# A second level of seven products for the down projection, and the next block's attention normed during the up phase

## The chip, the cores and the metric

The kernel runs on one core of a Trainium2 chip. Its measure is device time in microseconds; 1023.92 us is the median of three runs before the change.

## What is computed

Linear attention over 8 batches and 8 heads, then a gated feed-forward layer over all 4608 tokens.

```python
# q, k, v: (8, 8, 576, 64); x: (4608, 512); w_gate, w_val: (512, 1536); w_out: (1536, 512)
kv = np.einsum('bhsd,bhse->bhde', k, v)
o = np.einsum('bhsd,bhde->bhse', q, kv)
o = o / np.sqrt(np.mean(o * o, axis=-1, keepdims=True) + 1e-06) * g_norm
x = o.transpose(0, 2, 1, 3).reshape(4608, 512)
g = x @ w_gate
out = (g * (1.0 / (1.0 + np.exp(-g))) * (x @ w_val)) @ w_out
```

Everything is float32.

## The kernel before, in words

The 4608 tokens are worked in NB = 9 blocks of 512, numbered 0 to 8. A block has an up phase (x times w_gate and w_val, giving the hidden h, 1536 columns) and a down phase (h times w_out). Both use a seven-product scheme (Winograd's form of Strassen's): a 2x2 block product takes 7 block matmuls instead of 8, for additions of blocks on the other engines. The products are numbered 1 to 7. `CHAIN` says into which PSUM bank each goes: 1, 6, 7 and 4 add up one after another in one tile of pool b, each partial sum being copied out before the next product is added; 5 and 3 share a tile of pool c; 2 has pool a. The pools have 3, 2 and 1 banks, and pool m has the last 2, for attention.

From block DEEP = 2 on the up phase uses the scheme twice, an outer 7 of an inner 7 (class `Inner`). It goes through the 1536 hidden columns in three thirds d = 0, 1, 2. A third is four units, one for each group of outer products (`GROUPS`: 1 and 5; 6 and 2; 7; 4 and 3), so there are 12 units; each runs the inner products 1, 5, 6, 2, 7 and, while the next unit has begun, 3 and 4. Results of the first group leave PSUM by ScalarE copies or VectorE additions, those of the other groups by VectorE additions alone (L111 in the profile, the helper `add`). `made3` ends a third: two multiplications make h (L113), and `h_sums` makes the sums that the down phase needs, on GpSimd for d = 0 and 1, on VectorE for d = 2.

Weight combinations of the up phase that are not kept in SBUF were written to DRAM in block 1. The class `Stream` brings them back through a pool of nine t tiles (`t_pool`): `pump` issues a load on SP's queue whenever the ninth tile back has been used. `use` and `free` count the uses.

The down phase (class `Down`) uses one level: 7 products of 12 matmuls, 128x256 each (L565, the matmul of `Quad`). Three of its weight combinations are made on GpSimd into t tiles (`turn_t`, L112 t<-wo), nine operations a block. 

The next block's attention is done alongside. `kv` (L316) runs at one third and two thirds of the up phase. `turn` transposes q on VectorE (L331) after the up phase; `steps` gives what is done after which down product. For block 1 and later: after product 1, `whole`, which is the products q times kv (`heads`, L361), squares on ScalarE (L374), reductions on VectorE (L375), an inverse root of small VectorE operations (`root`, L381 to L393), `scale` (L113 r<-m,y) and the 32x32 transposes of `blocks_x` (L420); after product 5, `place_x`, 16 DMAs with 128-byte rows (L434), 8 on SP's queue and 8 on ScalarE's; after product 2, `gain_x` on ScalarE (L441) and `sums` on VectorE (L111, L112 on x and xi). Loads of k, v and q for the block after the next are issued on SP's queue; q of one block is 32 DMAs of 128-byte rows (L284).

Results and intermediate blocks of 128x2048 share five `ring()` buffers; x, xi, h and s1 have one buffer each. The text gives each engine's work an order of preference, and the Tile scheduler lays out every engine's list in advance: the first instruction in the text whose inputs and buffers it expects to be ready goes next. [...]

## Time and profile before

| | before |
|---|---|
| median of 3 runs | 1023.92 us (1023.57 to 1023.99) |
| profiled execution, first to last instruction (span) | 1021.4 us |
| TensorE busy | 1006.0 us, 98% |
| VectorE busy | 701.1 us, 69% |
| GpSimd busy | 369.0 us, 36% |
| ScalarE busy | 227.9 us, 22% |
| DMA, mean over the span | 167 GB/s |
| one block, 2 to 5, start of down to start of next down | 107.8 us |

The profile is of one execution; the profiled execution's own time is its span, with what lies before the first and after the last instruction outside it. Engines: PE is TensorE's matmul side, PEld its weight loads, DVE VectorE, ACT ScalarE, POOL GpSimd, SP the queue that issues most DMAs. In a row of the time line stand the start in us, the time, the engine, the line, the operation, what is written and read, shapes and the number of merged instructions; in brackets the idle time before it and what ended it. The chain of work that ended last gives start, time and engine. The clock granted to TensorE is full throughout.

### The profile page before, as it was taken

The page shows a single profiled execution, that of the slowest core. Times are in us where ns is not written, and L with a number is a line of the kernel's source. Part 1 is how long each engine was busy: PE and PEld are TensorE (multiplying, and loading weights), DVE is VectorE, ACT ScalarE, POOL GpSimd, SP SyncE. Part 2 cuts the span into 40 slices and gives each one's busy share as a digit, 9 for nine tenths or more (in the row PEclk, how much of TensorE's full clock was granted, in tenths as well). Part 3 has the DMA queues.
Part 4 walks back from the last instruction along what each step waited for, and adds up shares of the span by engine and source line. Part 5 has one row for each costly group of instructions (what it writes and reads, how often), then busy time and mean ns, then how long its engine had stood idle before and what let it go on. Part 6 is the DMA issues. An engine that isn't in the chain of part 4 may idle for free.

```text
span 1021.4 us, 21409 instructions
## 1 busy us (share of the span) xinstructions
PE 1006.0 (98%) x8522; PEld 897.1 (88%) x8522; DVE 701.1 (69%) x1169; ACT 227.9 (22%) x353; POOL 369.0 (36%) x280
## 2 busy tenths in 40 slices
PE   6999999999999999999999999999999999999998
PEld 4544688888999989998999899988998999989997
DVE  2999688998665946685558566665669466946661
ACT  2765112121211221121121211111121211221110
POOL 0000263534055503561246315630555045513670
PEclk9999999999999999999999999999999999999999
DMA  8689643767888377845686568636772766066601
GB/s 237 203 255 271 124 77 108 187 165 156 250 210 255 60 176 203 252 92 129 209 238 144 96 195 247 177 60 201 231 199 46 177 195 190 22 167 201 191 27 42
DMA packets 273845, 170.26 MB, mean 167 GB/s; under 512 B 150609, under 2 KB 241873, under 8 KB 273745
## 3 DMA queue, kind: packets, MB, share of 16 engines
q1 hardware_dynamic: 238800, 164.42, 59.3%
q10 hardware_dynamic: 34880, 4.46, 2.7%
q8 instruction: 68, 1.11, 0.4%
q14 instruction: 33, 0.26, 0.1%
q0 software_dynamic: 64, 0.00, 0.0%
HBM read 138.02 MB, written 22.41 MB: 157 GB/s over the span
## 4 chain that ended last, share of the span: by engine, by line
PE 90%; DVE 6%; DMA 2%; issue 1%; ACT 1%; SPq 0%; DVEq 0%; ACTq 0%
PE b L728 26%; PE b L565 19%; PE c L728 13%; PE c L565 10%; PE a L728 6%; PE a L565 5%; PE b L1032 4%; PE c L1032 4%; PE m L316 2%; PE m L361 1%; DVE r L112 1%; DVE xi L112 1%; DVE r L111 1%; DMA h<-in_v_dram 1%; DVE t L112 1%
## 5 line engine op out<-in xcount | busy, mean ns | idle before, releaser
L111 POOL TENSOR_TENSOR r<-r 128x256 f32<-128x256 f32 (+1 forms) x105 | 110.8, 1061 | 300.9 <-DVE r L111 272.2
L111 DVE TENSOR_TENSOR r<-b,r 128x512 f32<-128x512 f32 (+1 forms) x273 | 161.9, 606 | 65.5 <-PE b L728 60.1
L112 POOL TENSOR_TENSOR t<-wo 128x512 f32<-128x512 f32 x81 | 114.5, 1438 | 212.4 <-DVE wo L111 102.9
L111 DVE TENSOR_TENSOR r<-c,r 128x512 f32<-128x512 f32 (+1 forms) x179 | 108.5, 617 | 89.0 <-PE c L728 54.8
L728 PE MATMUL b<-x,t 128*128 128x128 f32 x1092 | 151.3, 276 | 0.0
L111 DVE TENSOR_TENSOR r<-a,r 128x512 f32<-128x512 f32 (+1 forms) x99 | 62.5, 631 | 113.4 <-PE a L565 70.7
L728 PEld LDWEIGHTS b<-x,t 128*128 128x128 f32 x1092 | 136.5, 192 | 0.8
L728 PE MATMUL c<-xi,t 128*128 128x128 f32 x840 | 112.4, 276 | 0.4 <-DVE xi L111 0.4
L113 POOL TENSOR_TENSOR h<-r 128x1024 f32<-128x1024 f32 (+1 forms) x40 | 82.3, 2072 | 76.9 <-DVE r L111 73.9
L728 PEld LDWEIGHTS c<-xi,t 128*128 128x128 f32 x840 | 102.9, 192 | 0.5 <-DVE xi L111 0.5
L565 PE MATMUL b<-wo,h 128*128 128x256 f32 x432 | 100.1, 383 | 0.1
L565 PE MATMUL b<-t,h 128*128 128x256 f32 x432 | 96.9, 381 | 0.0
L565 PEld LDWEIGHTS b<-t,h 128*128 128x128 f32 x432 | 81.6, 190 | 11.3 <-issue 0.2
L565 PEld LDWEIGHTS b<-wo,h 128*128 128x128 f32 x432 | 79.9, 190 | 13.1 <-DVE h L113 2.5
L742 ACT COPY r<-b 128x512 f32<-128x512 f32 x63 | 36.9, 585 | 211.6 <-PE b L728 211.6
L728 PE MATMUL b<-xi,t 128*128 128x128 f32 x588 | 79.8, 276 | 0.0
L728 PEld LDWEIGHTS b<-xi,t 128*128 128x128 f32 x588 | 72.4, 192 | 0.0
L728 PE MATMUL b<-x,wg 128*128 128x128 f32 x336 | 52.7, 279 | 0.2 <-DVE x L112 0.2
L728 PE MATMUL b<-x,wv 128*128 128x128 f32 x336 | 51.4, 276 | 0.0
L565 PE MATMUL a<-wo,h 128*128 128x256 f32 x216 | 48.3, 379 | 0.0
L565 PE MATMUL c<-t,s 128*128 128x256 f32 x216 | 48.1, 380 | 0.0
L565 PE MATMUL c<-wo,h 128*128 128x256 f32 x216 | 48.1, 379 | 0.0
(133 smaller groups left out, 1565.7 us busy)
## 6 DMA issues: line engine op xcount, KB each, us to landing
t<-w SPq DMA_DIRECT2D x336, 256.0 KB, 3.6
out_dram<-r SPq DMA_DIRECT2D x17, 512.0 KB, 3.1
ld<-in_k_dram SPq DMA_DIRECT2D x26, 288.0 KB, 5.2
ld<-in_v_dram SPq DMA_DIRECT2D x26, 288.0 KB, 5.9
ld<-in_moe_w_gate_dram SPq DMA_DIRECT2D x12, 512.0 KB, 4.8
ld<-in_moe_w_val_dram SPq DMA_DIRECT2D x12, 512.0 KB, 4.7
ld<-in_moe_w_out_dram SPq DMA_DIRECT2D x12, 512.0 KB, 4.9
w<-t SPq DMA_DIRECT2D x18, 256.0 KB, 3.0
```

The source lines that it names most:

```text
L111: add = lambda e, o, a, b: e.tensor_tensor(out=o, in0=a, in1=b, op=OP.add)
L112: sub = lambda e, o, a, b: e.tensor_tensor(out=o, in0=a, in1=b, op=OP.subtract)
L113: mul = lambda e, o, a, b: e.tensor_tensor(out=o, in0=a, in1=b, op=OP.mult)
L316: nc.tensor.matmul(self.kv_ps[r][u * D : (u + 1) * D, g, :], lhsT=k[:, u, c, :], rhs=v[:, u, c, :], start=(c == 0), stop=(c == KT - 1),)
L361: self.multiplied = nc.tensor.matmul(self.ps[i][u][p : p + D, t, j, :], lhsT=self.qt[rows, 2 * i + t, j, p : p + D], rhs=kvs[b % 3][rows, ...
L565: nc.tensor.matmul(banks[e][:, e], lhsT=lhsT, rhs=rhs, start=first and i == 0 and (e == 0 or banks[0] is not banks[1]), stop=i == self.ste ...
L728: nc.tensor.matmul(ps[:, i, f], lhsT=self.weight(o, p, f), rhs=self.operand(o, p), start=first and (i, f) == (0, 0), stop=True, skip_group ...
L742: nc.scalar.copy(out=dst, in_=ps)
L1032: nc.tensor.matmul(t, lhsT=w[f // 2][:, i, P * (f % 2) : P * (f % 2 + 1)], rhs=x[:, i, of], start=(i == 0), stop=(i == NS - 1),)
```

## The change

With DEEPER = 3, blocks 3 to 8 take the down products by two levels: outer 7 of inner 7, each with three matmuls of 128x128 (over d), 147 in all, in three groups of outer products (1, 2 and 4; 6 and 5; 3 and 7). The class `DeepDown` does it. The operands need more sums of blocks of h (`turn_h`, and `leaf` on VectorE for the first group and on GpSimd for the others); results are put together by VectorE, ScalarE and GpSimd (`row`). Weights: the combinations of the outer products 4, 5 and 7 are made once, on GpSimd in block 2 (`send_t`), written to DRAM and streamed back through the t tiles, 21 loads a block; those of the resident outer products are partly made on GpSimd each time (`get_down`, 12 a block) after wo was prepared in block 3. `turn_t` is not called from block 3 on.

For the next block (4 to 8) `turn` moves to the two-thirds point of up, and the steps of `whole` are split over the last third of up (`early`): the first half's products and root after unit 9 of 12, its scaling and the second half's products and root after unit 10, the second scaling after 11, `blocks_x` after 12. The squares are put into t tiles instead of a ring buffer. `place_x` and `end` stay in the down phase, in the first and the second group.

```diff
-            if i == 0:
+            early = self.n > DEEPER
+            if i == 0 and not early:
                 self.sq = ring().rearrange("p f (t j d) -> p f t j d", t=2, j=NS)
             for u in range(2):
-                sq = self.sq[:, 2 * i + u]
+                if early:
+                    sq = t_tile((self.n, "sq", i, u)).rearrange("p a (t x) -> p (a t x)", t=2)
+                    sq = sq.rearrange("p (t j d) -> p t j d", t=2, j=NS)
+                else:
+                    sq = self.sq[:, 2 * i + u]
                 self.squared = nc.scalar.activation(out=sq, in_=self.ps[i][u], func=ACT.Square)
                 self.summed = nc.vector.tensor_reduce(out=self.z[:, i, u], in_=sq, axis=mybir.AxisListType.X, op=OP.add)
+                if early:
+                    stream.free((self.n, "sq", i, u))
...
+        def early(self):
+            def first():
+                self.product(0)
+                self.root(0)
+            def second():
+                self.scale(0)
+                self.product(1)
+                self.root(1)
+            return {9: first, 10: second, 11: lambda: self.scale(1), 12: self.blocks_x}
...
+            if self.n > DEEPER:
+                return {5: self.place_x, 2: end}
...
+            if self.ffn.n >= DEEPER:
+                self.ffn.turn_h(self.d, engine)
+            else:
+                self.ffn.ended = self.ffn.h_sums(2 * self.d, 2, engine)
...
+    DEEPER = 3
+    DOWN = (((1, 2, 4), (1, 5, 2, 6, 3, 7, 4)), ((6, 5), (1, 5, 6, 3, 2, 7, 4)), ((3, 7), (1, 5, 6, 3, 2, 7, 4)))
+    DOWN_LEAVES = (1, 6, 2, 3, 4, 5, 7)
+    PLACE = {1: (0, 0), 2: (1, 0), 6: (0, 1), 3: (1, 1)}
+    wos = wo.rearrange("p (d m e) (g c x) -> p d m e g c x", m=2, e=2, g=2, c=2)
...
+                if n >= DEEPER:
+                    self.next += [
+                        (n, o, p, None) for os, ps in DOWN for p in ps for o in os
+                        if o not in RESIDENT or p not in QUARTER
+                    ]
...
+                if len(key) == 4:
+                    self.tiles[key] = t_tile(key).rearrange("p l (f c) -> p (l f) c", f=2)
+                    self.uses[key] = NP // 2
+                    self.get_down(self.tiles[key][:, 0 : NP // 2], *key[1:3])
+                    continue
...
+        def get_down(self, to, o, p):
+            if o in RESIDENT:
+                e, g = PLACE[o]
+                m, c = {5: (1, 1), 7: (0, 0), 4: (1, 0)}[p]
+                sub(nc.gpsimd, to, wos[:, :, m, e, g, c], wos[:, :, 0, e, g, 1])
+            else:
+                nc.sync.dma_start(out=to, in_=self.down[o][:, DOWN_LEAVES.index(p)])
...
+        def send_t(self, o):
+            if o == 4:
+                room = s_pool.tile([P, NP, HB], F32, name="s1").rearrange("p j (r t) -> p (j r) t", t=P)
+            else:
+                if o == 5:
+                    self.leaves = x_pool.tile([P, 3, 7, P], F32, name="xi").rearrange("p a b c -> p (a b) c")
+                room = self.leaves[:, 9 * (o == 7) :]
+            e = nc.gpsimd
+            for d in range(NP // 2):
+                t = self.turned_t[o][d].rearrange("p m (c x) -> p m c x", c=2)
+                t2_, to = t[:, 0, 1], room[:, 3 * d : 3 * d + 3]
+                sub(e, t2_, t[:, 1, 1], t2_)
+                add(e, t2_, t2_, t[:, 0, 0])
+                sub(e, to[:, 0:2], t[:, 1], t2_.unsqueeze(1).to_broadcast([P, 2, P]))
+                sub(e, to[:, 2], t[:, 0, 0], t2_)
+                down = stream.down[o]
+                nc.sync.dma_start(out=down[:, 0:4, d], in_=t.rearrange("p m c x -> p (m c) x"))
+                nc.sync.dma_start(out=down[:, 4:7, d], in_=to)
+            stream.free((self.ffn.n, o))
...
+    class DeepDown:
...
+        MADE = {1: (0, 0), 5: (1, 1), 6: (0, 1), 4: (1, 0)}
+        ADDED = {2: (0, 0), 7: (1, 1), 3: (0, 1)}
...
+        def multiply(self, group, p, ds=(0, 1, 2)):
+            outers = DOWN[group][0]
+            name, first = CHAIN[p]
+            if first and ds[0] == 0:
+                self.ps[name] = PSUMS[name].tile([P, 4, P], F32, name=name)
+            ps = self.ps[name][:, 0 : len(outers)]
+            for i, o in enumerate(outers):
+                for d in ds:
+                    nc.tensor.matmul(
+                        ps[:, i], lhsT=self.operand(o, p, d), rhs=self.weight(o, p, d),
+                        start=first and (i, d) == (0, 0), stop=d == 2, skip_group_check=True,
+                    )
+            if ds[-1] == 2:
+                q, c = (self.ADDED if p in self.ADDED else self.MADE)[p]
+                dst = (self.r[:, 0:3], self.r[:, 0:4:3], self.o)[group][:, :, q, c]
+                if p in self.ADDED:
+                    add(nc.vector, dst, ps, dst)
+                elif group == 0:
+                    nc.scalar.copy(out=dst, in_=ps)
+                elif group == 1:
+                    add(nc.vector, dst[:, 0], ps[:, 0], dst[:, 0])
+                    nc.scalar.copy(out=dst[:, 1], in_=ps[:, 1])
+                else:
+                    add(nc.vector, dst, ps, self.r[:, 0:1, q, c].to_broadcast([P, 2, P]))
+            stream.pump()
...
+        def go(self, nxt):
+            fill = nxt.steps() if nxt else {}
+            fill = {k: fill.get(k, lambda: None) for k in (1, 5, 2)}
+            h, r, forms = self.h, self.r, self.forms
+            vector, pool_ = nc.vector, nc.gpsimd
+            final = nxt is None
+            stream.enable(self.n + 1)
+            for p in (1, 5, 2):
+                self.multiply(0, p, (0, 1))
+            self.multiply(0, 1, (2,))
+            with tc.issue_after(self.ffn.ended.ins):
+                self.multiply(0, 2, (2,))
+            self.multiply(0, 5, (2,))
+            room = x_pool.tile([P, 7, 2, HB], F32, name="x").rearrange("p a b (c t) -> p (a b c) t", t=P)
+            for p in (3, 7):
+                to = room[:, 9 * (p == 7) :][:, 0:9].rearrange("p (o d) t -> p o d t", o=3)
+                self.leaf(
+                    vector, p, to[:, 0:2].rearrange("p o d t -> p d o t"), lambda m, q: h[:, :, m, :, 0, q]
+                )
+                self.leaf(vector, p, to[:, 2], lambda m, q: h[:, :, m, 1, 1, q])
+                for i, o in enumerate((1, 2, 4)):
+                    forms[o, p] = to[:, i]
+            self.multiply(0, 6)
+            self.multiply(0, 3)
+            self.row(pool_, add, 1, r[:, 1], r[:, 0], 0)
+            self.s1 = s_pool.tile([P, NP, HB], F32, name="s1")
+            pairs = self.ffn.h.rearrange("p (j e) t -> p e j t", e=2)
+            a11, a12, a21, a22 = (pairs[:, e, :, HB * g : HB * (g + 1)] for g in range(2) for e in range(2))
+            add(vector, self.s1, a21, a11)
+            s1 = self.s1.rearrange("p (d m) (q t) -> p d m q t", m=2, q=2)
+            xi = x_pool.tile([P, 3, 7, P], F32, name="xi").rearrange("p a b c -> p (a b) c")
+            for i, p in enumerate((5, 3, 7)):
+                for k, of in ((6, lambda m, q: h[:, :, m, 0, 1, q]), (5, lambda m, q: s1[:, :, m, q])):
+                    at = 6 * i + 3 * (k == 5)
+                    forms[k, p] = xi[:, at : at + 3]
+                    self.leaf(pool_, p, forms[k, p], of)
+            self.multiply(0, 7)
+            fill[5]()
+            self.multiply(0, 4)
+            self.row(pool_, add, 1, r[:, 1], r[:, 0], 1)
+            if final:
+                self.store(r[:, 1], 0, 0)
+            sub(vector, a11, a21, a22)
+            sub(vector, a12, a12, a21)
+            for p in (1, 5, 6, 3, 2):
+                self.multiply(1, p)
+            self.row(pool_, add, 0, r[:, 0], r[:, 3], 0)
+            fill[2]()
+            self.multiply(1, 7)
+            self.multiply(1, 4)
+            self.row(pool_, add, 0, r[:, 0], r[:, 3], 1)
+            sub(pool_, r[:, 2], r[:, 2], r[:, 3])
+            for p, to in ((5, h[:, :, 0, 1, 1]), (3, h[:, :, 0, 0, 1]), (7, h[:, :, 1, 1, 1])):
+                self.leaf(pool_, p, to, lambda m, q: h[:, :, m, :, 0, q])
+                forms[7, p], forms[3, p] = to[:, :, 0], to[:, :, 1]
+            self.o = self.quads(ring())[:, 0:2]
+            for p in (1, 5, 6, 3, 2):
+                self.multiply(2, p)
+            engine = vector if final else pool_
+            self.row(engine, add, 2, self.o[:, 1], r[:, 2], 0)
+            if final:
+                self.store(self.o[:, :, 0], 0, 1, 2)
+                self.store(r[:, 2, 0:1], 2, 0)
+            self.multiply(2, 7)
+            self.multiply(2, 4)
+            self.row(engine, add, 2, self.o[:, 1], r[:, 2], 1)
+            if final:
+                self.store(self.o[:, :, 1], 1, 1, 2)
+                self.store(r[:, 2, 1:2], 3, 0)
+            else:
+                self.store(self.o.rearrange("p o q c t -> p (o q) c t"), 0, 1)
+                self.store(r[:, 1:3].rearrange("p o q c t -> p (o q) c t"), 0, 0)
...
+        def turn_h(self, d, engine):
+            h = self.h.rearrange("p (d m e) (g q t) -> p d m e g q t", m=2, e=2, g=2, q=2)[:, d]
+            outer = self.h.rearrange("p (j e) t -> p e j t", e=2)[:, :, 2 * d : 2 * d + 2]
+            a11, a21, a22 = outer[:, 0, :, 0:HB], outer[:, 0, :, HB:BLK], outer[:, 1, :, HB:BLK]
+            s2 = h[:, 0, :, :, 1]
+            add(engine, s2, s2, h[:, 1, :, :, 1])
+            sub(engine, s2, s2, h[:, 0, :, :, 0])
+            to = self.s1.rearrange("p j (r t) -> p (j r) t", t=P)[:, 0:9].rearrange("p (o d) t -> p d o t", o=3)[:, d]
+            add(engine, to[:, 0:2], h[:, 0, :, 0, 1], h[:, 0, :, 0, 0])
+            self.ended = add(engine, to[:, 2], h[:, 0, 1, 1, 1], h[:, 0, 1, 1, 0])
+            add(engine, a21, a21, a22)
+            return sub(engine, a21, a21, a11)
...
+            if self.n == DEEPER:
+                for d in range(NP // 2):
+                    of = lambda m, c, d=d: wos[:, d, m, :, :, c]
+                    self.making += [
+                        lambda of=of: sub(nc.gpsimd, of(0, 1), of(1, 1), of(0, 1)),
+                        lambda of=of: add(nc.gpsimd, of(0, 1), of(0, 1), of(0, 0)),
+                    ]
...
+                if self.n == DEEPER - 1 and p in (5, 7, 4):
+                    down.send_t(p)
...
-                nxt.kv(0)
+                with tc.issue_after(ffn.multiplied.ins) if n >= DEEPER else ExitStack():
+                    nxt.kv(0)
                 nxt.load_kv(1)
             def two_thirds():
                 nxt.kv(1)
+                if n >= DEEPER:
+                    nxt.turn()
...
+            if nxt and n >= DEEPER:
+                fill.update(nxt.early())
             ffn.up(fill)
-        if nxt:
+        if nxt and n < DEEPER:
             nxt.turn()
         if 0 < n < NB - 2:
```

## Prediction

> **What bounds the kernel now.** I read the shares of busy time first, then the chain of work that ended last, then the groups of instructions, and last the time line of one block's end (block 5, up phase ending at 664.4 us).
>
> The page's first part:
>
> ```profile
> PE 1006.0 (98%) x8522; PEld 897.1 (88%) x8522; DVE 701.1 (69%) x1169; ACT 227.9 (22%) x353; POOL 369.0 (36%) x280
> ```
>
> TensorE has 15 us of idle time in 1021. A gain must shorten its own work; a loss comes from whatever makes it wait. In the chain, pieces of the down products (L565) and of the up products (L728) give their pace:
>
> ```profile
> 568.29 5.18 PE c L565 x24
> ...
> 602.31 1.79 PE b L728 x16
> ```
>
> A matmul is two records. A 128x256 record takes 5.18/24 = 0.2158 us, a 128x128 record 1.79/16 = 0.1117 us. The second is 4% dearer per column.
>
> VectorE is the engine to watch. Its time line, where up turns into down:
>
> ```profile
> 661.19 1.23 DVE L331 STREAM_TRANSPOSE r<-ld 128x1024 f32<-128x1024 f32 x1
> ...
> 664.55 0.69 DVE L111 TENSOR_TENSOR r<-b,r 128x512 f32<-128x512 f32 x1 [0.96 <-PE b L728]
> ...
> 665.35 2.36 DVE L113 TENSOR_TENSOR h<-r 128x1024 f32<-128x1024 f32 x2
> ...
> 670.94 2.46 DVE L375 TENSOR_REDUCE z<-r 128x8 f32<-128x512 f32 x4
> 673.44 1.22 DVE L381 TENSOR_SCALAR z<-z 128x32 f32<-128x32 f32 x1
> ...
> 676.72 0.19 DVE L393 SCALAR_TENSOR_TENSOR y<-a,y 128x32 f32<-128x32 f32 x1
> ...
> 679.42 2.36 DVE L420 STREAM_TRANSPOSE r<-r 128x1024 f32<-128x1024 f32 x2
> ```
>
> The next block's norm fills VectorE from 670.94 to 681.8, 10.8 us on end, at a place where the old down products ask almost nothing of it. The stretches of the last third of up say how much room there is instead (PE, PEld, DVE, ACT, POOL busy):
>
> ```profile
> 647.00:664.40 17.40, 17.40 (x152) 17.24 (x151) 13.60 (x23) 1.64 (x2) 13.94 (x12) 1.00 0.58 136
> ```
>
> VectorE is 78% busy there, GpSimd 80%.
>
> [...] no POOL row has a PSUM operand. [...] L381 takes 1.22 us on 32 elements while POOL runs to 674.6, L384 after it 0.18.
>
> **The change, part by part.**
>
> *Down products, blocks 3 to 8.* Out go 7x12 = 84 matmuls of 128x256: 84x2x0.2158 = 36.3 us. In come 7x7x3 = 147 of 128x128: 147x2x0.1117 = 32.8. Gain 3.4 per block, 20.5 in all six. This lies on the path, as L728's pace with the same two operand shapes shows.
>
> *The attention of the next block, blocks 3 to 7.* Its TensorE products (668.55 to 670.58, 2.0 us) and the ScalarE squares (4x0.6) only move. On VectorE the four reductions, the root, four scalings and two transposes move too, and the root runs twice: 673.44 to 676.95, 3.5 us more, so 10.8+3.5 = 14.3. The transposes of q (2.4 us) move to the two-thirds mark, where there is room. Now the room. From the end of the first unit of the last third, VectorE must do 13.6-2.4 = 11.2 of evictions, these 14.3, and the last eviction and two multiplications that make h (664.55 to 667.71, 3.2): 28.7; closely packed evictions start 0.60 apart instead of 0.69, so about 27.8. In that time TensorE has 17.4 of up products, 2.0 of attention and, before it needs the last third of h, 18 down matmuls, 18x2x0.1117 = 4.0: together 23.4. **It waits about 4.4 us.** The evictions are queued behind the norm on VectorE, and every bank's next product waits for one; the scheduler places work in the order of the text, in which the norm stands before the last unit. The same sum for the kernel before gives 16.8 needed in 20.9, no wait, as traced. Bounds: about 1.5, if the two x transposes (2.4) fall behind the making of h and L381 meets an idle POOL; 7, if the squares wait a microsecond for their t tiles and L381 and L384 wait for 2.4 us POOL operations. A gain is excluded.
>
> *Between h and the first second-level products.* The last turn_h on VectorE adds two 512 operations, a 256 and a 128 one, then two leaves of 768+384 elements[...]. With h at 3.3 us after the last up product, product 5's operand is there at about 5.3, where TensorE comes at 5.4, and product 3's at about 8.4 against 8.0. I take 0.6 us; 0.2 to 1.5.
>
> *GpSimd in the down phase.* Out: nine t<-wo (9x1.44 = 12.9). In: 12 weight differences of 384 elements (between the 0.74 of 256 and 1.44 of 512: 1.05), six row sums of 256 (0.74), six leaves of 384, one sum of 512 (1.3) and three leaves of 768 (about 1.85): 30 us in a phase of 33. The leaves of groups two and three still come some 2 us ahead of their products, if the weight differences don't stall the queue: 0, bounds 0 to 2. In the up phase turn_h grows from 2.5 to about 6.3 us for each of two thirds; 13.9+3.8 of 19.4 us, hidden.
>
> *Weights on SP's queue.* Each down phase now takes 33 t tiles, 21 loaded (192 KB) and 12 made on POOL, where before all nine were made. Nine slots at one tile a microsecond are 9 us ahead; a load of 256 KB lands in 3.6. But place_x stands in the same queue:
>
> ```profile
> 658.86 26.26 SPq L284 DMA_DIRECT2D ld<-in_q_dram  x32
> 685.23 5.76 SPq L434 DMA_DIRECT2D x<-r  x8
> ```
>
> Its eight issues close SP for 5.8 us, released at about 12.1 us of the down phase, when group one's product 7 lets go of the x buffer; a tile behind it lands some 9 us later. I take 0.7 us of waiting, 0 to 3. The q loads, 0.6 us an issue (seven in 4.20 from 559.93), move forward with the earlier turn and fit between the up tiles, one of which comes per 1.4 us. x itself: 12.1+5.8, landing 3.3, gain 2.2, sums 9.0 (700.41 to 709.4 before) end at 32.4 of 32.8. Before, TensorE waited 0.5 us there (707.29); that goes.
>
> *Once.* Block 2 makes and writes the second-level weights: 36 POOL operations (three of 128, about 0.45, and one of 256, nine times: 18.8 us) and 18 writes; its nine t slots come free up to 8 us later, just ahead of block 3's use. Block 3's up makes six sums on POOL. I take 0.5; 0 to 5. Block 8 has no next attention: -3.4+0.6, and at the very end product 4 follows 7 in one bank (an eviction, about 0.7) and a row sum of 0.3 follows: -1.8.
>
> **The sum.** Blocks 3 to 7: -3.4-0.5+4.4+0.6+0.7 = +1.8 each, +9.0. With -1.8 and +0.5: +7.7. The profiled span is 1021.4 us; the timed median, 1023.9, is 2.5 above it for what lies around the span, and I leave that as it is: **1031.6 us**.
>
> **The rivals.** *Forecast (0.50 with its own spread):* VectorE can't hold the norm beside the evictions. For: 78% busy already. Against: the estimate assumes no slack is found.
> *The norm fits better (0.28), faster:* blocks_x waits for a ring buffer that only made2's POOL sum frees near the end of up, so it can fall behind the making of h. Then the wait is about 1.6, with 0.3 for leaves and 0.3 for weights: -1.7 in five blocks, -2.2 and +0.3: 1013.5. The sign turns where VectorE's wait falls below 4.4-1.5 = 2.9 us a block, since 5x0.3 then balances -1.8+0.5.
> *Weights late (0.15), slower still:* POOL's weight differences wait for slots at the head of an in-order queue, the row sums and leaves behind them come late, or tiles wait behind place_x: the upper bound of 3 us more in each of five blocks, 1046.6. Against: DMA is half idle in the old down phase.
> *Within 0.2% (0.05):* the ends meet. That the products don't fall as counted isn't open: they follow from the loops.
>
> **The numbers.** Slower than 0.2% (about 2 us, what a measurement of this kernel can tell): 0.50+0.15 and the slower part of what lies between, 0.67; faster 0.28; same 0.05. The range takes in the faster case with its spread, down to 1009, and the late weights, up to 1047. Forecast alone: 1023 to 1040.
>
> **What would show it.** Down records: 294 of 0.112 us per block, no L565 after block 2. VectorE above 90% in the last 20 us of up, gaps of TensorE there and at the first products on d=2, released by DVE: about 4 to 5 us a block in 3 to 7, under 1 in block 8. POOL near 90% in the down phase with no PE wait on it. I am wrong if the block period (107.8 now) falls below 106, if the waits are for DMA t tiles or POOL, or if the transposes of x stand after the multiplications that make h.

## The result, and the profile after

The changed kernel takes 1151.63 us (median of 3, 1148.84 to 1152.78) where the kernel before took 1023.92: a ratio of 1.1241, 95% interval 1.1217 to 1.1265. The forecast of 1031.6 had the direction right and the size wrong: 7.7 us were expected and 127.7 measured, some 17 times as much. The profiled execution has a span of 1151.0 us.

The first two parts of the page of the changed kernel, the row of engines and the clock granted to TensorE in 40 slices:

```profile
PE 1038.3 (90%) x9278; PEld 940.8 (82%) x9278; DVE 833.0 (72%) x1362; ACT 231.6 (20%) x377; POOL 568.5 (49%) x482
...
PEclk9999999999999998989998999989989999999999
```

TensorE goes from 98% to 90%; GpSimd's work grows by 200 us, VectorE's by 132. The clock, full throughout before, now has pieces at half, 64.9 us in all from block 3 on.

The matmuls themselves do what was forecast. From the chain of work that ended last, changed kernel (start, time, engine, line, count), a piece of down products at half clock after a wait, and two undisturbed ones:

```profile
754.14 1.29 PE b L1073 x6
...
1141.86 1.34 PE a L1073 x12
1143.20 1.35 PE b L1073 x12
```

1.34/12 = 0.112 us a record, as L728 had before; 1.29/6 = 0.215 at half clock. So the loss is waiting, and the half clock that follows it. I take each stretch's time over pace: from the start of one matmul to the start of the next, less what that shape takes when nothing waits (0.112 us here), added up; half clock counts in it. In blocks 3 to 7 the last third of up is 9.6 us over pace on average (before 0.06) and the down phase 17.9 us (before 1.8). The period of a block goes from 107.8 to 132.4 us (start of down of block 4 to that of block 5).

The last third of up, seen in the stretches of the changed kernel (start and end, length, busy time and count of PE, PEld, DVE, ACT, POOL, then clock, DMA share, GB/s), and then the whole down phase of block 4, with the same phase of the kernel before under it:

```profile
570.00:598.40 28.40, 23.12 (x234) 22.04 (x234) 25.39 (x51) 3.75 (x6) 16.86 (x16) 0.94 0.53 130
```

```profile
598.41:647.78 49.37, 35.44 (x271) 33.14 (x269) 33.70 (x42) 6.01 (x11) 29.73 (x24) 0.93 0.50 117
```

```profile
556.55:594.95 38.40, 38.38 (x326) 33.20 (x325) 24.19 (x36) 7.66 (x11) 9.05 (x6) 1.00 0.54 117
```

VectorE is at 25.4 of 28.4 us at the end of up: the forecast bottleneck. In the down phase neither VectorE (33.7 of 49.4) nor GpSimd (29.7) is full, and TensorE waits all the same: each of the two waits for the other, in chains that the rows further down show.

VectorE's time line at the end of up in block 4 shows what the root became. Before, its first operation took 1.22 us and each of the others 0.18 to 0.19:

```profile
591.99 0.16 DVE L398 SCALAR_TENSOR_TENSOR a<-y 128x16 f32<-128x16 f32 x1
592.08 0.68 DVE L111 TENSOR_TENSOR r<-b,r 128x512 f32<-128x512 f32 x1
592.68 1.92 DVE L399 TENSOR_TENSOR a<-a,z 128x16 f32<-128x16 f32 x1
594.52 0.68 DVE L111 TENSOR_TENSOR r<-a,r 128x512 f32<-128x512 f32 x1
```

GpSimd in the same microseconds, and TensorE a little later:

```profile
592.21 2.35 POOL L111 TENSOR_TENSOR r<-r 128x1024 f32<-128x1024 f32 x1 [2.28 <-DVE a L398]
```

```profile
597.42 1.16 PE L753 MATMUL b<-x,t 128*128 128x128 f32 x8 [1.63 <-DVE r L111]
```

Sixteen elements take 1.92 us, to 594.60, while GpSimd's 1024-element sum runs from 592.21 to 594.56. What stands behind in VectorE's list comes later, an eviction of bank b (from 596.69) among it, and TensorE waits 1.63 us for that bank.

In the down phase, TensorE, GpSimd and VectorE of block 4 in turn (in brackets the idle time before, and what ended it):

```profile
618.53 1.65 PE L1073 MATMUL c<-t,xi 128*128 128x128 f32 x6 [5.77 <-POOL t L112]
...
629.31 0.94 PE L1073 MATMUL b<-wo,h 128*128 128x128 f32 x6 [1.23 <-ACT r L1086]
632.15 0.94 PE L1073 MATMUL c<-wo,xi 128*128 128x128 f32 x6 [1.23 <-ACT r L1086]
```

```profile
607.31 1.65 POOL L111 TENSOR_TENSOR xi<-h 128x384 f32<-128x384 f32 x1 [7.65 <-DVE h L112]
608.91 2.98 POOL L112 TENSOR_TENSOR xi<-h 128x384 f32<-128x384 f32 x2
611.86 3.77 POOL L112 TENSOR_TENSOR t<-wo 128x384 f32<-128x384 f32 x2
615.59 0.99 POOL L111 TENSOR_TENSOR xi<-s 128x384 f32<-128x384 f32 x1
616.54 0.99 POOL L112 TENSOR_TENSOR xi<-s 128x384 f32<-128x384 f32 x1
617.49 0.99 POOL L112 TENSOR_TENSOR t<-wo 128x384 f32<-128x384 f32 x1
```

```profile
607.15 5.16 DVE L112 TENSOR_TENSOR x<-h 128x768 f32<-128x768 f32 x4
612.23 2.54 DVE L111 TENSOR_TENSOR s<-h 128x1536 f32<-128x1536 f32 x1
```

GpSimd idles 7.65 us until VectorE's last `turn_h` sum; then seven operations stand ahead of the weight difference for which TensorE waits 5.77 us. A 384-element operation takes 0.99 us alone; the five that meet VectorE's sums take 8.40. VectorE's four leaves (two of 768 elements, two of 384) take 5.16, where an estimate gives 3.0: on the line through 0.69 us for 512 elements and 1.76 for 1536, both in the kernel before, they are 2 x (0.96+0.56). The waits for ScalarE (L1086) are of another kind: its list holds 7.0 us of `place_x` issues there, from 621.49, and the evictions stand behind them.

### The profile page after: what moved, and what is told of

It is laid out like the page before. It is cut to its first block, busy times and chain, and to the rows that moved or that the text cites. A ratio compares the mean times of both kernels' runs of the same rounds, so it can differ in the third digit from the quotient of the medians.

```text
span 1151.0 us, 23739 instructions
## 1 busy us (share of the span) xinstructions
PE 1038.3 (90%) x9278; PEld 940.8 (82%) x9278; DVE 833.0 (72%) x1362; ACT 231.6 (20%) x377; POOL 568.5 (49%) x482
## 4 chain that ended last, share of the span: by engine, by line
PE 64%; DVE 21%; DMA 5%; issue 4%; POOL 3%; ACTq 1%; ACT 1%; POOLq 0%; SPq 0%; DVEq 0%
PE b L753 21%; PE c L753 10%; PE b L590 7%; PE a L753 5%; DVE r L111 5%; PE c L590 4%; PE b L1309 3%; PE c L1309 3%; PE b L1073 3%; DVE x L112 3%; PE m L361 2%; DVE xi L112 2%; PE a L590 2%; PE c L1073 2%; DMA x<-r 2%
## 5 line engine op out<-in xcount | busy, mean ns | idle before, releaser
L111 DVE TENSOR_TENSOR r<-b,r 128x512 f32<-128x512 f32 (+2 forms) x327 | 183.0, 568 | 108.9 <-PE b L753 58.6
L112 POOL TENSOR_TENSOR t<-wo 128x384 f32<-128x384 f32 (+1 forms) x99 | 125.1, 1279 | 186.8 <-DVE wo L111 104.4
L111 DVE TENSOR_TENSOR r<-c,r 128x512 f32<-128x512 f32 (+2 forms) x195 | 112.9, 586 | 71.9 <-PE c L753 51.2
L753 PEld LDWEIGHTS b<-x,t 128*128 128x128 f32 x1092 | 139.8, 196 | 27.5 <-DVE r L111 26.5
L111 DVE TENSOR_TENSOR r<-a,r 128x512 f32<-128x512 f32 (+2 forms) x111 | 66.5, 599 | 68.8 <-PE a L753 37.8
L1073 PE MATMUL b<-wo,h 128*128 128x128 f32 x288 | 46.2, 299 | 21.9 <-ACT r L1086 8.3
L1073 PE MATMUL b<-t,h 128*128 128x128 f32 x432 | 60.2, 283 | 4.8 <-DVE r L111 3.4
L1073 PEld LDWEIGHTS b<-wo,h 128*128 128x128 f32 x288 | 39.2, 206 | 26.0 <-ACT r L1086 9.3
L1073 PEld LDWEIGHTS b<-t,h 128*128 128x128 f32 x432 | 53.3, 194 | 8.4 <-DVE r L111 3.0
L112 POOL TENSOR_TENSOR h<-h 128x512 f32<-128x512 f32 (+1 forms) x36 | 52.3, 1454 | 1.9
L112 DVE TENSOR_TENSOR h<-h 128x1536 f32<-128x1536 f32 (+1 forms) x30 | 45.2, 1522 | 6.9 <-PE b L1073 5.7
L111 POOL TENSOR_TENSOR h<-h 128x512 f32<-128x512 f32 (+1 forms) x30 | 41.3, 1375 | 14.0 <-DVE h L112 13.1
```

What stands on the lines that cost most here:

```text
L111: add = lambda e, o, a, b: e.tensor_tensor(out=o, in0=a, in1=b, op=OP.add)
L112: sub = lambda e, o, a, b: e.tensor_tensor(out=o, in0=a, in1=b, op=OP.subtract)
L753: self.ffn.multiplied = nc.tensor.matmul(ps[:, i, f], lhsT=self.weight(o, p, f), rhs=self.operand(o, p), start=first and (i, f) == (0, 0), ...
L1073: nc.tensor.matmul(ps[:, i], lhsT=self.operand(o, p, d), rhs=self.weight(o, p, d), start=first and (i, d) == (0, 0), stop=d == 2, skip_gro ...
```

## The experiments

Each is one kernel, timed twice beside the kernel before on the same chip (1023.6 to 1024.6 us). Many leave work out and so compute something else; what each leaves out is said. Times over pace are means in us over blocks 3 to 7.

| kernel | us | ratio, 95% interval | last third of up | down |
|---|---|---|---|---|
| before | 1023.9 | | 0.06 | 1.8 |
| changed | 1151.6 | 1.1217 to 1.1265 | 9.6 | 17.9 |
| a_attn_only | 1048.0 | 1.0209 to 1.0269 | 6.65 | 0.03 |
| h_attn_quiet_pool | 1037.1 | 1.0101 to 1.0161 | 4.2 | 0.03 |
| n_deep_only | 1127.0 | 1.0976 to 1.1040 | 0.04 | 21.7 |
| b_no_root | 1121.2 | 1.0922 to 1.0985 | 2.8 | 18.2 |
| c_weights_dma | 1106.6 | 1.0740 to 1.0883 | 8.5 | 11.1 |
| m_sums_out_only | 1121.1 | 1.0919 to 1.0982 | 9.6 | 10.6 |
| o_no_gpsimd_sums | 1125.2 | 1.0941 to 1.1029 | 9.9 | 12.6 |
| g_dma_no_root | 1076.0 | 1.0481 to 1.0542 | 2.8 | 10.1 |
| j_no_vector_sums | 1059.5 | 1.0306 to 1.0386 | 2.8 | 6.8 |
| p_none | 1032.1 | 1.0047 to 1.0106 | 2.8 | 2.3 |
| d_dve_sums_act | 1152.0 | 1.1222 to 1.1287 | 9.8 | 18.9 |
| e_dma_place_sync | 1122.5 | 1.0934 to 1.0998 | 8.0 | 13.3 |
| f_leaves_late | 1146.4 | 1.1167 to 1.1232 | 9.7 | 16.5 |
| i_evict_vector | 1086.6 | 1.0579 to 1.0642 | 2.8 | 11.4 |
| k_both | 1059.1 | 1.0292 to 1.0393 | 2.8 | 6.5 |
| l_sends_behind_x | 1150.7 | 1.1193 to 1.1281 | 9.9 | 17.7 |

**The two parts apart.** a_attn_only keeps the old down products:

```diff
     DEEPER = 3
+    DOWNS = 99
-            if self.ffn.n >= DEEPER:      # in made3, and so wherever the down products are chosen
+            if self.ffn.n >= DOWNS:
```

The share theory of the expectations is that VectorE and GpSimd keep each other waiting, as in the 1.92 us for 16 elements above, which end at 594.60 where GpSimd's sum ends at 594.56.

> The attention of blocks 4 to 8 moves into the last third of up, the down products stay on one level. Share theory[...]: the root's small operations still meet the two multiplications of 2.4 us that GpSimd does for h, so TensorE waits 3 to 6 us in each of five last thirds; the down phase is free of VectorE work and gains nothing: 1035 to 1055 us. Overload theory (VectorE's operations are too many by count, no exclusion needed): 4.4 us a block as forecast, 1045. Down theory (the last third only shows what the down phase does to it): no wait above 1 us, 1024.

It takes 24 us more than the kernel before, 4.8 in each of five blocks, all of it in up. n_deep_only is the counterpart:

```diff
+    EARLY = 99
-            early = self.n > DEEPER       # and so wherever the norm is placed
+            early = self.n > EARLY
...
             self.multiply(0, 5, (2,))
+            fill[1]()
```

> The other part of the change alone, against a_attn_only: the down products by the second level from block 3 on, with GpSimd's differences, but the next block's attention product, norm and transposes left where the kernel before has them, in the down phase. If the two parts cost what they cost apart: 1151.6 less the 24 us that a_attn_only cost, 1124 to 1132, with last thirds at pace. If the down phase has no room for the norm beside its sums: 1140 to 1165, with down phases 5 us or more longer than the changed kernel's. If early attention is what makes the second level cost so much (both crowd VectorE at the end of the up phase): below 1110.

It is 24.6 us faster than the changed kernel, so 1127.0+1048.0-1023.9 = 1151.1: the parts add up, and about four fifths of the loss go with the second level. That the sum is so exact is partly luck, since n's waits are not the same: with the norm in the down phase, TensorE waits 8.4 us ahead of `kv` in each of blocks 3, 4 and 5, for a bank that the scaling frees.

**The root.** b_no_root:

```diff
             z = self.z[:, i : i + k]
+            if self.n > DEEPER:
+                self.y = self.z
+                return
```

> The changed kernel with the root of the early norm left out (the scale is taken from the sum of squares itself, 22 small VectorE operations a block fewer); all else stays. Overload theory: 7.0 us less VectorE work by the row durations of the kernel before, so the waits of about 8 us in each of five last thirds fall to about 1: 35 us less, 1115. Share theory: the same or a little more goes, 1105 to 1115, since the root's operations are the ones that are held up by GpSimd. If the waits there come from elsewhere (t tiles for the squares, the order of the list): 1140 or more.

30.5 us go, 6.1 a block, nearly all from the last third; the down phase stays. h_attn_quiet_pool asks why 22 small operations cost that, on the kernel with early attention alone:

```diff
-            add(nc.gpsimd, self.shared[2][:, 1, :, e, q], u2[:, :, e, q], r5[:, :, e, q])
+            if self.d == 2 and self.ffn.n >= DEEPER:
+                nc.scalar.copy(out=self.shared[2][:, 1, :, e, q], in_=u2[:, :, e, q])
+            else:
+                add(nc.gpsimd, self.shared[2][:, 1, :, e, q], u2[:, :, e, q], r5[:, :, e, q])
```

(and the same in `made2`.)

> On top of a_attn_only (early attention, the old down products; 1048.0 us), GpSimd's five sums in the last third of each up phase from block 3 on become ScalarE copies of one operand (the other operand is left out), so that GpSimd is idle while VectorE norms. In a_attn_only the 22 operations of the root take some 0.16 us each where GpSimd is idle and 0.3 to 1.9 us where one of its sums overlaps, about 7.7 us a block instead of 3.5. If this stretching is the loss: 3 to 4 us a block less, 1028 to 1034, and every operation of the root at 0.16 to 0.2 us. If it is the number of VectorE's operations between two evictions: 1044 to 1050, with short roots and the same waits.

10.9 us went, 2.2 a block, so both expectations missed. The root's operations of blocks 3 to 7 sum to 44.3 us in a_attn_only and 30.9 here, 13.4 less. They are not all short, since some GpSimd operations (sums of h of the second third, `turn_t`) still overlap; and only operations that overlap are long. From its time line:

```profile
548.83 0.83 DVE L391 TENSOR_SCALAR y<-z 128x16 int32<-128x16 int32 x1
549.69 0.18 DVE L398 SCALAR_TENSOR_TENSOR a<-y 128x16 f32<-128x16 f32 x1
549.90 0.17 DVE L399 TENSOR_TENSOR a<-a,z 128x16 f32<-128x16 f32 x1
550.11 0.17 DVE L400 SCALAR_TENSOR_TENSOR y<-a,y 128x16 f32<-128x16 f32 x1
```

GpSimd's last sum before it ends at 549.6. In this kernel, a_attn_only and the changed one, no operation of the root without such an overlap took over 0.18 us. Of the 4.2 us that remain, some is still this overlap (25 of the 110 operations take 0.32 us or more), the rest presumably the norm's length beside the evictions; no run divides them. In the changed kernel 2.8 us stay without any root.

**GpSimd's weight differences.** c_weights_dma:

```diff
-                sub(nc.gpsimd, to, wos[:, :, m, e, g, c], wos[:, :, 0, e, g, 1])
+                nc.sync.dma_start(out=to, in_=self.down[4][:, DOWN_LEAVES.index(p)])
```

> The 12 weight differences that GpSimd makes in each down phase are loaded instead from a stored combination (of other values, so the products are other ones; same shapes). Queue theory (GpSimd's in-order list in the down phase is too long): the wait of 2 to 8 us before product 5 of group two goes, and with it the half clock that follows; 6 to 10 us a block in six blocks, 1095 to 1115. Share theory: [...]the wait shrinks to the sums' own time, 1110 to 1130. Late-weights theory (the loads stand behind place_x on SP): slower than the changed kernel, 1155 or more.

45 us go, 7.5 in each of six blocks. g_dma_no_root has both edits:

> b_no_root and c_weights_dma together (the root of the early norm is left out, y = z, and the weight differences are loads of another stored combination). Alone they took 30.5 and 45 us off the 1151.6. If the two losses are separate places of the block: 75.5 off, 1076. If both were mostly the same time at half clock, which then counts once: 1085 to 1095. If the clock recovers more than either alone gave: below 1072.

1076.0, the plain sum: two separate places. Is it the order of GpSimd's list? f_leaves_late:

```diff
+            with tc.issue_after(stream.differ[6, 5].ins):
                 for i, p in enumerate((5, 3, 7)):
                     for k, of in (...):
                         self.leaf(pool_, p, forms[k, p], of)
```

> The changed kernel with one thing moved: GpSimd's six sums into xi (operands of the second group) are put behind the weight difference of outer 6, product 5 in GpSimd's list; the same work is computed. In the changed kernel two differences stand ahead of the first of these sums in blocks 3 to 5, where TensorE waits 4.0, 5.9 and 7.9 us for a difference at product 5, and four in blocks 6 and 7, where it waits 2.2 us each. If it is the order of the list (a sum at its head waits for h while differences that could be made stand behind it): these 22 us go, or most of them, with some time at half clock behind them, 1120 to 1135. If it is the amount of GpSimd's work: the wait moves to the sums themselves and the time stays within 5 us of 1151.6.

Only 5 us. The order matters little: the wait goes over to the sums that were put behind, 12.1 us in four waits where 21.5 in five stood for the differences. Its TensorE, block 4:

```profile
614.82 0.80 PE L1073 MATMUL c<-t,xi 128*128 128x128 f32 x2 [3.03 <-POOL xi L111]
```

**The sums of h.** d_dve_sums_act took VectorE's to ScalarE:

```diff
-            add(vector, self.s1, a21, a11)
+            nc.scalar.copy(out=self.s1, in_=a21)
```

(and so for the two leaves and the two sums behind.)

> VectorE's sums of h in the down phase (two leaves, s1, the differences in a11 and a12) become plain copies of the same size on ScalarE, which changes the operands' values; GpSimd's work stays. Share theory: GpSimd's 384-element operations in the first 15 us of the down phase go back from 1.5 to 1.9 us to 1.0, the wait before product 5 of group two falls from about 6 us to under 3: 1110 to 1130. Queue theory: GpSimd's list is as long as before, the wait stays within a microsecond: 1140 to 1150.

The time did not change. GpSimd's operations went back to 1.00 us, yet in block 4 the wait for the weight difference at product 5 fell only from 5.77 to 4.87 us (over all blocks from 21.5 to 13.9): there the late start and the length of GpSimd's list weigh more than the stretching. What was gained is lost again because two copies stand in ScalarE's list behind `place_x`, and TensorE waits 4.9 us for them in block 4 (PE b<-wo,h for ACT h), 28.4 in all. The later kernels leave the sums out instead. m_sums_out_only:

```diff
-                self.leaf(vector, p, to[:, 2], lambda m, q: h[:, :, m, 1, 1, q])
-            add(vector, self.s1, a21, a11)
-            sub(vector, a11, a21, a22)
-            sub(vector, a12, a12, a21)
```

> The changed kernel with only the edit of j_no_vector_sums: VectorE's sums of h inside the down phase are left out (readers take plain parts of h), while GpSimd computes the weight differences and VectorE the root as in the changed kernel. In j_no_vector_sums this took 16.5 us off a kernel whose weight differences were loads. If VectorE's sums and GpSimd's differences are two separate queues with their own waits: again 14 to 20 us off 1151.6, 1132 to 1138, with the wait for a weight difference at product 5 still 4 us or more. If the differences are late because GpSimd's operations are stretched beside VectorE's sums: over 30 us off, below 1122, and that wait gone.

30.5 us, the size of the second expectation, but the wait that should have gone with it is still there, 17.9 us in six waits against 21.5 in five: the differences are late for their own reasons too. The 30.5 us are not the sums' alone. The two leaves lay in the x buffer that `place_x` fills, and without them ScalarE begins to issue `place_x` 2.9 us into block 4's down phase, not 23.1, ahead of the evictions that stood behind. Block 8 places nothing; there the edit takes 2.2 us off the down phase (from 9.8 to 7.5 over pace). How the rest divides was not tested. On top of g_dma_no_root the same edit gave 16.5:

> On top of g_dma_no_root: VectorE's sums of h inside the down phase (operands of the first group's products 3 and 7, s1, and the two that remake the outer a11 and a12) are left out, and their readers take plain parts of h. TensorE waits some 1.0, 0.8 and 1.7 us a block at such sums or at VectorE evictions behind them in blocks 3 to 7, and 1.4 in block 8. If these sums are the rest of the down phase's loss: 16 to 22 us less, 1054 to 1060, down phases with 6 us of idle instead of 10. If the evictions on ScalarE are the whole of it: 1070 to 1076.

o_no_gpsimd_sums leaves out GpSimd's:

```diff
-                    self.leaf(pool_, p, forms[k, p], of)
+                    forms[k, p] = of(0, 0)
```

> The changed kernel without GpSimd's sums of h in the down phase (six into xi for the second group, three into h for the third): their readers take plain parts of h. The twelve weight differences, VectorE's sums and the root stay. f_leaves_late showed TensorE's wait at product 5 to move from a difference to one of these sums when the two change places. If it is the amount of GpSimd's work in the down phase: 15 to 30 us less, 1122 to 1137. If only the differences count: 1145 or more. If VectorE's sums were stretched mostly by these operations (1.35 us for 384 elements[...]): below 1122, with the sums near 0.6 us.

26.5 us less. The same instructions of VectorE as above, in this kernel:

```profile
602.91 2.75 DVE L112 TENSOR_TENSOR x<-h 128x768 f32<-128x768 f32 x4
605.58 1.75 DVE L111 TENSOR_TENSOR s<-h 128x1536 f32<-128x1536 f32 x1
```

2.75 us in place of 5.16, 1.75 in place of 2.54: the estimate of 3.0 is near what the leaves took without GpSimd's sums, and far from what they took beside them (last section).

**Two ways round `place_x`.** The waits under ScalarE's name pointed at its issues. e_dma_place_sync (on c_weights_dma):

```diff
-                    queue = nc.scalar if b % 2 else nc.sync
+                    queue = nc.sync
```

> On top of c_weights_dma (twelve weight differences of a block loaded instead of computed, so the numbers of those products are not the reference's), all 16 transfers of place_x are issued on SP's queue and none on ScalarE's. In c_weights_dma, which took 1106.6 us, two pairs of ScalarE evictions of the second group stand behind 7 us of issues and TensorE waits 2.1 and 1.4 us for them in each of blocks 3 to 7. If those issues are the cause: 3.5 us x 5 = 17.5 less, 1086 to 1092, and block 8, which places nothing, keeps its 4.1 us of idle. If 16 issues in a row on SP make the weights or x late: 1104 or more, with waits for DMAs in place of those for ScalarE.

16 us slower than c_weights_dma, some of it in blocks that the change leaves alone. The issues did hold the evictions: in block 4 the two waits fell from 1.9 and 1.3 us to 0.5 and 0.1. But the weights come late behind 16 issues on SP, as the second expectation had it: a wait of 3.4 us for a load appeared in block 4, and such waits (b for DMA t<-d) sum to 20.2 us. i_evict_vector (on g_dma_no_root):

```diff
-                    nc.scalar.copy(out=dst[:, 1], in_=ps[:, 1])
+                    nc.vector.tensor_copy(out=dst[:, 1], in_=ps[:, 1])
```

> On top of g_dma_no_root (1076.0 us; no root, weight differences loaded): the four ScalarE evictions of the second group's outer 5 in each block are made by VectorE instead, so that none stands behind the 7 us in which ScalarE issues place_x. If those issues hold the second group: the two waits of about 2.1 and 1.4 us in blocks 3 to 7 go, 17 us less, 1058 to 1064. If VectorE is what holds these evictions too, it has 0.4 us more to do at each and the waits stay under its name: 1072 or more.

11 us slower: in block 4 TensorE waits 4.0 us for a VectorE eviction instead. And k_both, with j's edit:

> i_evict_vector and j_no_vector_sums together on g_dma_no_root. If loads in place of the differences, no root, no VectorE sums in the down phase and no evictions behind place_x are the places of the loss: 1036 to 1044, with down phases within 4 us of their pace; what is left above the time before is then the start of block 3 (9 us) and 2.8 and 3 us of VectorE's norm and evictions in each up phase, against 20 us less of matmuls. If each cure only lets the next wait come forward: 1055 or more.

As j_no_vector_sums, where `place_x` is issued before these evictions anyway. So neither way round the issues was worth anything, because each put another wait in its place; what the issues cost by themselves stays open.

**All four at once.** p_none:

```diff
+            if self.n > DEEPER:                       # root: y = z
...
-            if o in RESIDENT and p in QUARTER:        # weight: no differences, no loads for them
+            if o in RESIDENT:
...
-                    self.leaf(pool_, p, forms[k, p], of)   # and VectorE's, as in m_sums_out_only
```

> The changed kernel with all of it left out at once: no root (y = z), no sums of h on VectorE or GpSimd in the down phase, and no weight differences (products 5, 7 and 4 of the resident outer products take a resident quarter of w_out, with no load in its place). The matmuls are the same. If these four are the places of the loss, what is left is the start of block 3 (9 us), some 2.8 and 3.0 us of norm and evictions in five up phases, against 20 us less of matmuls and 17 us of waits that the kernel before had: 1022 to 1032. If ScalarE's evictions behind place_x, or the loads of t<-d, are places of their own: 1038 or more, with waits under those names.

1032.1, at the edge of the first expectation: of the 127.7 us, 119.5 go with these four, and the down phase is 2.3 us over pace, though the evictions and 21 loads a block are all there. `place_x` is there too, but ScalarE begins to issue it 2.3 us into the down phase, as in m_sums_out_only, so this run does not clear its issues. Its block 4, down phase:

```profile
569.52:603.66 34.14, 32.56 (x285) 31.90 (x283) 18.07 (x31) 6.22 (x11) 4.13 (x5) 1.00 0.75 176
```

The four alone (b, c, m, o) sum to 132.5, 13 us more than together. Most of that lies between the sums on VectorE and the rest, since j's edit gave 30.5 alone and 16.5 behind the other two. None of the kernels is faster than the one before, p_none included, so taking these waits away would not by itself make the change pay.

**Block 3, once.** Its up phase is 20.1 us over pace, 8 more than block 4's. l_sends_behind_x:

```diff
+                with tc.issue_after(behind.ins):      # behind = nxt.placed
                     nc.sync.dma_start(out=down[:, 0:4, d], ...)
```

> The changed kernel with the once-only sending of the combined w_out put behind place_x on SP's queue in block 2; the same work. In the changed kernel SP's share of place_x is issued at 366.0 us, behind six sends that wait for GpSimd, though the transposed rows are ready at 359.3; the sums of x then start 5.8 us later than before and block 3's first two thirds lose some 9 us once. If the order on SP's queue is the cause: 5 to 12 us less, 1140 to 1147. If GpSimd's sums beside VectorE's sums of xi (2.1 us instead of 1.09) or late weights are the larger part: within 3 us of 1151.6.

`place_x` did move, from 366.0 to 359.5, and the first sums of x from 377.0 to 372.1. But the sums of xi still begin at 382.9 (383.2), and three of the four still take 1.5 to 2.2 us (1.09 before), GpSimd preparing wo beside them. The xi buffer is also where `send_t` puts part of what it writes out, and the last of these writes lands at 381.3 (381.9 in the changed kernel), just before those sums; whether that sets their start was not tested. Block 3's up gains 1.3 us. The rest of its 8 us was not tested either.

## Why the prediction was wrong, by its steps

The forecast's one large loss, the norm in the last third, is real but accounts for 24 of the 128 us. Most of the rest comes from GpSimd in the down phase, which it put at nothing, and from the sums behind h, which it put at 0.6 us a block.

**Down products, -3.4 a block.** Right: 294 records of 0.112 us.

**The norm in the last third, +4.4 in bounds 1.5 to 7, with -0.5 for the old wait.** Inside the bounds where it stands alone: 6.65 in the last third of a_attn_only, 4.8 a block net. The waits come from VectorE, as said. In the changed kernel the last third loses 9.6, above the upper bound, and the root alone is worth 6.1. Mis-sized is the term "the root runs twice ... 3.5 us more": that makes 7.0 a block with the pauses between operations, and in the changed kernel the operations alone sum to 52.0/5 = 10.4. The upper bound let two kinds (L381, L384) wait for GpSimd; beside it all five kinds took longer, 0.65 to 1.93 us at most by kind; the four that are also seen alone took 0.16 there.

**Between h and the first products, +0.6 in bounds 0.2 to 1.5.** Failed. The forecast's times for the leaves were an estimate with nothing of GpSimd beside them, some 3.0 us for the four (as on the line above); they took 5.16. And the step has no term for VectorE's three sums of 1536 elements behind them (s1 and the two differences), for which TensorE waits up to 3.0 us (block 7). Without leaves, s1 and differences 30.5/6 = 5.1 us a block go, `place_x`'s earlier start included; 2.2 in block 8, which has no `place_x`.

**GpSimd in the down phase, 0 in bounds 0 to 2.** Failed, the largest error. The 29.7 us busy in block 4 agree with the 30 forecast by luck: they are 24 of the 28 operations, some of them stretched. And the amount was compared with the length of the phase, as if GpSimd could start at its beginning; but it has to wait for h (7.65 us in block 4), with weight differences standing behind in its list (in f_leaves_late, where the sums stand behind one of them, two differences ran at 603.21 and 605.64, in what is idle time here), and its operations took longer beside the very VectorE sums that feed it. Left out, the differences give back 45/6 = 7.5 us a block and its sums 26.5/6 = 4.4. The stretching could be read before: the 1.44 us that the step takes for a 512-element operation is a mean over the kernel before, where in blocks 2 to 5 eight of nine take some 1.27 and one 2.86. That one, the first of the three merged here, starts beside a VectorE sum of h (block 5):

```profile
669.27 1.76 DVE L112 TENSOR_TENSOR h<-h 128x1536 f32<-128x1536 f32 x1
```

```profile
669.30 5.32 POOL L112 TENSOR_TENSOR t<-wo 128x512 f32<-128x512 f32 x3 [6.72 <-DVE h L112]
```

The forecast had one such time, L381's 1.22 us beside a running POOL, and carried it to the root alone, not to the sums of h.

**Weights on SP's queue, +0.7.** Small, as forecast: waits for t<-d stay under 0.8 us in block 4, and p_none, which keeps all 21 loads, has 0.9 us of them in all.

**Once, 0.5 in bounds 0 to 5.** Too small: 8, above the upper bound; the cause is in part open.

**Block 8, -1.8.** Wrong in sign for the same reasons: up and down go from 102.1 to 110.0 us; in p_none they are 101.2.

**What no step had: half clock.** The forecast's waits were counted once, at a full clock. In the changed kernel's trace the clock is at half in 14 pieces of 3.41 or 6.83 us, and each has TensorE idle ahead of it, though seldom throughout: in the 3.41 us before a piece it idled 1.76 us or more 13 times, and 1.35 once. The 64.9 us at half clock are up to 32 us of the loss (an estimate: half of them), on top of the waits ahead of them. Waiting alone need not bring it: a_attn_only, which is 6.65 us over pace in a last third, had a granted clock of 1.0 (1.00 in 544.50:570.08, TensorE busy for 22.43 of these 25.58 us). What decides it was not shown.

The rival "weights late" came nearest: an in-order queue of GpSimd, held at its head, with what stands behind it late. But it named the wrong holder (free slots; in block 4 it is h, for 7.65 us) and gave it at most 3 us a block. Of what was to show the forecast wrong, waits for POOL came true with 21.5 us. Of what was to show it right, VectorE's share at the end of up came near (89%, 25.39 of 28.40 us, for "above 90%"), and "POOL near 90% in the down phase with no PE wait on it" failed (29.73 of 49.37 us, 60%).

## What to carry to other kernels

Work that is moved to VectorE and GpSimd at once isn't hidden by two idle shares: where both read two operands from SBUF, each took longer beside the other (here a VectorE sum 1.35 us in place of 0.55, a GpSimd one up to 2.5 in place of 0.99). So add their times in the stretch where both are needed, instead of comparing each with the phase. Price a producer chain from the moment its input exists, through every list it stands in, not as a sum of busy time against the length of a phase. And a saving of 3.4 us a block in matmuls is used up by one wait of 3 us, if a piece of 3.41 us at half clock follows, as 9 of the 14 pieces here were (an estimate: 3 us, and half of 3.41).

## What the hardware showed that I had not expected

Changed kernel, blocks 3 to 8, VectorE with and without a GpSimd operation beside it:

- L400, two SBUF inputs of 16 elements: 0.157 to 0.161 us alone (10), 0.375 to 0.645 beside GpSimd (20). L399: up to 1.93.
- L391, one SBUF input and constants, 16 elements: 0.158 alone (2), 0.70 to 0.90 beside GpSimd (8).
- x<-h of 384 elements: 1.34 to 1.36 beside GpSimd (12); 0.54 to 0.55 alone (8, in o_no_gpsimd_sums).
- Evictions of 512 elements, one input in PSUM, one in SBUF (r<-b,r): 0.69 alone (55) and 0.69 beside GpSimd (107). Reductions (L380) 0.67 to 0.69 beside GpSimd, 32x32 transposes 1.23 either way.

So in this kernel operations of 16 elements took longer beside GpSimd too (60 of the root's 110 over 0.25 us, up to 1.93), and evictions, with one input in PSUM, did not: none of the 107 beside GpSimd took over 0.69. The long ones ended with GpSimd's: all these 60 end 0.03 to 0.04 us after the end of a GpSimd operation. On the other side a 384-element GpSimd operation of 0.99 us takes up to 2.5.
